# A linear-attention and gated-MLP kernel: when two weight loads, one query product and two blocks of h are issued

## The chip, the cores and the metric

The kernel runs on one core of a Trainium2 chip. The metric is device microseconds of one execution, the median of several runs. The core has a matrix engine (PE; its weight loads are listed as PEld), a vector engine (DVE), a scalar engine (ACT), GpSimd (POOL) and SyncE (SP). Each engine executes its own instructions in the order in which they were written. Here SP and ACT also issue DMAs: SP's run on queue q1, ACT's on q10, both on the core's 16 DMA engines.

## The reference

For x of 2048 x 576 (one batch), all in fp32:

```
phi(t) = where(t > 0, t + 1, exp(t)) + 1e-6
kv  = sum over s of phi(k)[s] v[s]          # 32 heads of 18
z   = sum over s of phi(k)[s]
a   = (phi(q) kv / (phi(q) z + 1e-6)) @ wo
b   = (gelu(x @ w_gate) * (x @ w_up)) @ w_down     # 576 -> 4608 -> 576
g   = sigmoid((x * gate_w).sum(-1))
out = g * a + (1 - g) * b
```

## The kernel before

**Arithmetic.** Every operand of a product is split in two parts, high and low; a product is three matmuls (high by high, high by low, low by high). The large products of the MLP follow a scheme of seven products for a 2 x 2 block product, with sums of blocks made beforehand; `f`, `e`, `u`, `p` are the buffers in which DVE combines the seven results.

**Stages.** Until about 134 us keys, values and their grams are made. Then `states` (L445 to L454) multiplies `wv` with the grams, for five slices kt; each slice needs its split of `wv`, the low part of which POOL makes (L424). `key_sums_mm` (L461 to L465) is ten matmuls with two columns each. `query(b, g)` (L427 to L437) is 14 matmuls 512 wide for block b and head group g, then two activations on ACT and one DVE operation. `wo_load` (L513) brings a slice of `wo`, splits it on ACT and POOL; `states_out` (L521) takes the states out of PSUM; the result meets `wo` at L551. Until 285 us PE does the attention: for each of 16 row tiles `mixed(b, t)` (L671) runs 30 matmuls on `p`, the split of scaled queries (`scaled`, L662 and L68/L69), for which DVE needs `rb`, the reciprocals of the denominators, stored to HBM (L646) and loaded back broadcast (L650) by SP. The result is copied by ACT to a buffer `ga` (L686) and stored on ACT's queue (L688); there are two `ga` buffers.

**Gate and up.** From 258 to 1109.5 us come 72 chains (`CHAINS`, `gu_steps`), numbered c0 to c71, gate or up, each seven products of seven matmuls (L828), 11.5 us. A chain other than the first runs its products in the order s1, s6, s7, s5, s2, s4, s3. The result of s1 is copied by ACT to `p` (L869); s2 accumulates on the same bank and so waits for that copy. s3 accumulates on s5's bank and waits for the DVE operation that reads it (L860 in a gate chain, L863 in an up chain). A gate chain writes `e` or `f`, with a GELU on ACT (L850, L880); an up chain multiplies into it (L853) and SP stores the blocks to `h_d` (L856). Gate weights are in `W[0]` (`wg`), up weights in `W[1]` (`wu`): the first ones are loaded ready-made from `wp_d` (2240 KB each), the later ones are fetched raw (`stage<-wgu`, L832), summed by POOL (L283) and split by ACT and POOL (`w_split`, L841 to L843). In chains 0 to 3, `s_make` (L1010 to L1014) splits sums of x that SP loads from `xsum_d` to `f` (L1008).

**Into the down stage.** With LAST = 71, chain LAST - 1 is the last gate chain (c70), LAST - 2 the last but one up chain (c69). Its weights for the last up chain (`last_up`, in the room of x's first blocks, printed as `xo`) are loaded on ACT's queue at c69 (L1047). The first down weights are fetched raw by `d_fetch(0)` (1728 KB, L971) and split by `d_make` (L977, L979). `h_load(j)` (L992, 768 KB) brings back a block of h from HBM on SP; `h_make(j)` (L997 ACT, L998 DVE) splits it. The tables `D_AT` and `H_AT` say behind which product (c, i) of the chain loop (L1028) these are issued; i counts from 0, so i = 1 is s6, i = 3 is s5, i = 5 is s4. From 1109.5 us the down stage (L1092) runs 84 units of 36 matmuls.

The order of instructions on each engine is the order of the program's text (a manual schedule).

## Time and profile before

| | |
|---|---|
| median of 3 runs | 1513.2 us (1511.0 to 1515.54) |
| profiled execution | 1515.58 us |
| its span in the trace | 1513.8 us |
| its mean granted PE clock | 0.996 |
| PE busy | 1500.9 us (99%) |
| DVE, POOL, ACT busy | 1003.3, 718.7, 546.2 us |
| PE's longest waits | 3.1 and 1.9 us for ACT's p, 0.8 for DVE's f |

In rows of the timeline the columns are start, duration, engine, line, operation, out<-in, shapes, and in brackets the idle time before the instruction with what ended it. A DMA's row on SPq or ACTq is its issue; in the chain of waits a DMA's row is the transfer up to its landing.

### The profile page before, as it was taken

The numbers are of one execution on the slowest core, as the hardware profiler recorded it, in microseconds if no ns is written. First come the engines' busy times: TensorE is split into PE (matmuls) and PEld (weight loads), VectorE is DVE, ScalarE is ACT, GpSimd is POOL, SyncE is SP. The second block draws the span as 40 slices with busy tenths as digits, with TensorE's granted clock in tenths as the row PEclk, the third lists the DMA queues.
The fourth block names the chain that finished last, engine by engine and source line by source line (L and its number), as shares of the span: only waits on it lengthen the run. The fifth ranks groups of instructions, "written<-read, shape, count | busy, mean of one in ns | idle before, by whom it ended". The sixth has DMA issues, their size and how long they took to land.

```text
span 1513.8 us, 21594 instructions
## 1 busy us (share of the span) xinstructions
PE 1500.9 (99%) x8354; PEld 1323.3 (87%) x8354; DVE 1003.3 (66%) x1324; ACT 546.2 (36%) x711; POOL 718.7 (47%) x516
## 2 busy tenths in 40 slices
PE   9999999999999999999999999999999999999999
PEld 8998889887888888888888888888789999999999
DVE  7886776385666556666556665556677767777775
ACT  6554545333222332222332222332244344444431
POOL 1674532156644644644644644543357354644620
PEclk9999999999999999999999999999999999999999
DMA  7563374662332223332223332223877656565564
GB/s 248 164 204 117 148 256 166 231 259 91 139 133 96 105 101 123 139 126 97 105 98 132 140 123 100 105 93 116 308 274 281 213 168 214 167 214 177 204 200 135
DMA packets 98494, 246.36 MB, mean 163 GB/s; under 512 B 9040, under 2 KB 36328, under 8 KB 95960
## 3 DMA queue, kind: packets, MB, share of 16 engines
q1 hardware_dynamic: 95368, 233.13, 44.2%
q10 hardware_dynamic: 3024, 11.86, 2.2%
q8 instruction: 65, 1.06, 0.3%
q14 instruction: 37, 0.30, 0.1%
HBM read 156.72 MB, written 88.24 MB: 162 GB/s over the span
## 4 chain that ended last, share of the span: by engine, by line
PE 91%; DVE 3%; issue 2%; ACT 2%; DMA 1%; POOL 1%; SPq 0%; ACTq 0%; POOLq 0%; DVEq 0%
PE bank L828 53%; PE bank L1092 26%; PE bank L433 3%; PE pair L681 2%; PE pair L199 2%; PE kpair L244 1%; PE pair L244 1%; PE kpair L199 1%; DMA ga_d<-ga 1%; POOL wv L424 1%; PE den L573 0%; DMA raw<-wk 0%; DVE f L853 0%; ACT p L68 0%; DVE r L662 0%
## 5 line engine op out<-in xcount | busy, mean ns | idle before, releaser
L828 PE MATMUL bank<-xo,wg 128*128 128x512 f32 x1764 | 414.3, 395 | 1.3 <-DVE f L860 0.8
L828 PE MATMUL bank<-xo,wu 128*128 128x512 f32 (+1 forms) x1715 | 403.4, 396 | 3.1 <-ACT p L869 3.1
L828 PEld LDWEIGHTS bank<-xo,wg 128*128 128x128 f32 x1764 | 332.1, 188 | 79.5 <-DVE e L860 1.4
L828 PEld LDWEIGHTS bank<-xo,wu 128*128 128x128 f32 (+1 forms) x1715 | 324.4, 189 | 79.0 <-ACT p L869 3.6
L1100 DVE SCALAR_TENSOR_TENSOR acc<-bank,gate,acc 128x288 f32<-128x288 f32 x288 | 140.5, 512 | 71.0 <-PE bank L1092 70.2
L283 POOL TENSOR_TENSOR stage<-stage 128x384 f32<-128x384 f32 x132 | 155.0, 1195 | 46.1 <-DMA stage<-wgu 43.5
L869 ACT ACTIVATE p<-bank 128x512 f32<-128x512 f32 x72 | 43.0, 597 | 333.9 <-PE bank L828 324.7
L842 POOL TENSOR_TENSOR wg<-stage,wg 128x768 fp32r<-128x768 f32 (+1 forms) x34 | 72.9, 2144 | 185.6 <-ACT wg L841 184.3
L842 POOL TENSOR_TENSOR wu<-stage,wu 128x768 fp32r<-128x768 f32 (+1 forms) x34 | 80.2, 2359 | 149.0 <-ACT wu L841 147.7
L1092 PE MATMUL bank<-wd,xo 128*128 128x288 f32 x1008 | 135.8, 294 | 0.0
L1092 PEld LDWEIGHTS bank<-wd,xo 128*128 128x128 f32 x1008 | 134.1, 188 | 0.0
L979 POOL TENSOR_TENSOR xo<-stage,xo 128x432 fp32r<-128x432 f32 x44 | 64.7, 1493 | 117.2 <-ACT xo L977 117.2
L874 DVE TENSOR_TENSOR u<-bank,p 128x512 f32<-128x512 f32 x72 | 49.5, 687 | 94.1 <-PE bank L828 88.8
L1092 PE MATMUL bank<-xo 128*128 128x288 f32 x792 | 107.1, 295 | 0.1
L1092 PEld LDWEIGHTS bank<-xo 128*128 128x128 f32 x792 | 105.7, 188 | 0.5 <-DVE u L863 0.4
L979 POOL TENSOR_TENSOR wd<-stage,wd 128x432 fp32r<-128x432 f32 x40 | 59.6, 1515 | 90.5 <-ACT wd L977 90.5
L860 DVE TENSOR_TENSOR f<-bank,u 128x512 f32<-128x512 f32 x54 | 37.3, 691 | 76.7 <-PE bank L828 76.5
L860 DVE TENSOR_TENSOR e<-bank,u 128x512 f32<-128x512 f32 x54 | 37.1, 691 | 74.1 <-PE bank L828 73.9
L850 ACT ACTIVATE f<-f 128x512 f32<-128x512 f32 x54 | 34.2, 633 | 143.8 <-DVE f L860 143.8
L984 POOL TENSOR_TENSOR stage<-stage 128x432 f32<-128x432 f32 x48 | 77.2, 1635 | 0.0
L888 DVE TENSOR_TENSOR u<-bank,u 128x512 f32<-128x512 f32 x72 | 49.8, 692 | 35.9 <-PE bank L828 33.6
L850 ACT ACTIVATE e<-e 128x512 f32<-128x512 f32 x54 | 34.1, 633 | 91.2 <-DVE e L860 90.8
(192 smaller groups left out, 2347.6 us busy)
## 6 DMA issues: line engine op xcount, KB each, us to landing
h_d<-sx SPq DMA_DIRECT2D x108, 256.0 KB
stage<-wgu SPq DMA_DIRECT2D x34, 768.0 KB
xo<-h_d SPq DMA_DIRECT2D x29, 768.0 KB
e<-h_d SPq DMA_DIRECT2D x28, 768.0 KB
hraw<-h_d SPq DMA_DIRECT2D x27, 768.0 KB
h_d<-e SPq DMA_DIRECT2D x72, 256.0 KB
h_d<-f SPq DMA_DIRECT2D x72, 256.0 KB
stage<-wdn SPq DMA_DIRECT2D x6, 1728.0 KB
```

The lines of the kernel that those rows point to most:

```text
L199: nc.tensor.matmul(out_t[:, :n], xa, kvw[i][:rows, r, lo:lo + n], start=(k == 0), stop=(k == 13))
L283: nc.gpsimd.tensor_tensor(o, a, b, OP.subtract)
L828: nc.tensor.matmul(ps, w_, x_, start=start and i == 0, stop=i == 6, skip_group_check=not start)
L842: nc.gpsimd.tensor_tensor(w[:, i, 3:5], src[:, :, 0:2], f32(w[:, i, 0:2]), OP.subtract)
L850: nc.scalar.activation(es[i], es[i], AF.Gelu_apprx_tanh)
L860: nc.vector.tensor_tensor(es[i], a, b, OP.add)
L874: nc.vector.tensor_tensor(u2, b, p1, OP.add)
L888: nc.vector.tensor_tensor(u3, c, u2, OP.add)
L979: nc.gpsimd.tensor_tensor(w[:, 1, c], src[:, c], f32(w[:, 0, c]), OP.subtract)
L984: nc.gpsimd.tensor_tensor(draw[:, o, c], draw[:, x, c], draw[:, y, c], OP.subtract)
L1092: nc.tensor.matmul(y, h[:, hl, g, t * 128:(t + 1) * 128], w[:, wl, g * 288:(g + 1) * 288], start=k in (1, 5) and n == 0, stop=n == len(ops ...
L1100: nc.vector.scalar_tensor_tensor(o, y, gate[:, 1, st:st + 1], o, op0=OP.mult, op1=OP.add)
```

## The change

There are four edits. `query(2, 3)` moves from behind the two `wo_load` calls to between `states(3)` and `states(4)`. The load of the first up weights into `W[1]` moves from ACT's queue, behind the first `mixed(1, t)`, to SP's, right behind the last load of reciprocals. In `H_AT` the splits of the first two h blocks move from behind s5 and s4 of the last gate chain to behind s6 and s5, and the load of the second h block moves four products later in c69. `d_fetch(0)` moves from the second product of c68 to the first of c67.

```
--- before.py
+++ after.py
@@ -490,8 +490,10 @@
     nc.vector.reciprocal(gate[:, 0], gate[:, 0])
     nc.vector.tensor_scalar(gate[:, 1], gate[:, 0], -1.0, 1.0, op0=OP.mult, op1=OP.add)
     query(2, 2)
-    for kt in range(2, 5):
-        states(kt)
+    states(2)
+    states(3)
+    query(2, 3)
+    states(4)
     key_sums_mm(rs)
     made.close()
     values.close()
@@ -575,7 +577,6 @@
 
     wo_load(0)
     wo_load(1)
-    query(2, 3)
     states_out()
     key_sums()
     query(2, 4)
@@ -805,6 +806,7 @@
     scaled_parts(0, 3)
     reciprocal(1, 1)
     reciprocals_load(1, 1)
+    nc.sync.dma_start(f32(W[1]), wp_d[1])
     mixed(0, 2)
 
 
@@ -928,8 +930,6 @@
     for t in range(BT):
         if t + 1 < BT:
             scaled(1, t + 1)
-        if t == 1:
-            nc.scalar.dma_start(f32(W[1]), wp_d[1])
         mixed(1, t)
     mixing.close()
     first_pairs.close()
@@ -1020,7 +1020,7 @@
     D_AT = {(LAST - 2, 0): lambda: d_make(0, 0), (LAST - 2, 4): lambda: d_sum(T1), (LAST - 1, 0): lambda: d_sum(T2),
             (LAST - 1, 2): lambda: d_make(0, 1), (LAST - 1, 4): lambda: d_make(0, 2), (LAST - 1, 6): lambda: d_sum(T3),
             (LAST, 4): lambda: d_sum(T4)}
-    H_AT = [(LAST - 1, 3), (LAST - 1, 5)]
+    H_AT = [(LAST - 1, 1), (LAST - 1, 3)]
     at = {}
     for n in range(1, NF2):
         for m in range(2):
@@ -1045,11 +1045,10 @@
                 nc.sync.dma_start(f32(W[0]), wp_d[0])
             if i == 0 and c == LAST - 2:
                 nc.scalar.dma_start(f32(last_up), wp_d[1])
-            if (c, i) == (LAST - 3, 1):
+            if (c, i) == (LAST - 4, 0):
                 d_fetch(0)
-            if (c, i) == (LAST - 2, 0):
-                h_load(0)
-                h_load(1)
+            if c == LAST - 2 and i in (0, 4):
+                h_load(i // 4)
             if (c, i) in D_AT:
                 D_AT[c, i]()
             if (c, i) in H_AT:
```

On PE, behind the fourth slice of the states (`pair<-gt,wv` and `bank<-gt,wv` are states, `bank<-xo,qw` a query, `bank<-ones,rs` the key sums), before:

```order
L454 MATMUL pair<-gt,wv 126x126
L452 MATMUL bank<-gt,wv 72x144
L454 MATMUL bank<-gt,wv 72x72
L465 MATMUL bank<-ones,rs 126x2 x8
L465 MATMUL bank<-ones,rs 72x2 x2
L433 MATMUL bank<-xo,qw_121 126x512 x7
L433 MATMUL bank<-xo,qw_122 126x512 x7
L433 MATMUL bank<-xo,qw_121 72x512 x7
L433 MATMUL bank<-xo,qw_122 72x512 x7
```

and in the change:

```order
L454 MATMUL pair<-gt,wv 126x126
L452 MATMUL bank<-gt,wv 72x144
L454 MATMUL bank<-gt,wv 72x72
L433 MATMUL bank<-xo,qw_121 126x512 x7
L433 MATMUL bank<-xo,qw_122 126x512 x7
L452 MATMUL pair<-gt,wv 126x252
```

The 14 matmuls of `query(2,3)`, the first two query rows, have moved from behind the key sums to ahead of the last slice of the states.

On SP, at the last loads of reciprocals (`rb`), before:

```order
L650 DMA rb<-rden_d_66 126x1x1280
L646 DMA rden_d_67<-rb 35x256
L650 DMA rb<-rden_d_67 126x1x1280
L1008 DMA f<-xsum_d_73 128x1024
L1008 DMA f<-xsum_d_74 128x1024
L832 DMA stage<-wgu 128x1536
L1008 DMA f<-xsum_d_75 128x1024
```

and in the change:

```order
L651 DMA rb<-rden_d_66 126x1x1280
L647 DMA rden_d_67<-rb 35x256
L651 DMA rb<-rden_d_67 126x1x1280
L809 DMA wu<-wp_d_97 128x4480
L1008 DMA f<-xsum_d_73 128x1024
L1008 DMA f<-xsum_d_74 128x1024
L834 DMA stage<-wgu 128x1536
L1008 DMA f<-xsum_d_75 128x1024
```

The load `wu<-wp_d` now stands between the reciprocals and the loads of `f`; on ACT's queue, where it stood between a split of `p` and the next `ga` copy, it is gone.

On SP, at the end of c69's predecessor and in c69 (`e_3197` is the second raw buffer of h, `sx` and `f` are stored blocks of an up chain), before:

```order
L1045 DMA wg<-wp_d_96 128x4480
L971 DMA stage<-wdn 128x3456
L856 DMA h_d_5_103<-e_3197 128x512
L856 DMA h_d_5_103<-e_2873 128x512
L856 DMA h_d_5_103<-sx 128x512 x2
L856 DMA h_d_5_103<-e_3197 128x512 x2
L856 DMA h_d_5_103<-sx 128x512
L992 DMA xo<-h_d_1_99 128x1536
L992 DMA e_3197<-h_d_1_99 128x1536
L856 DMA h_d_5_109<-f 128x512 x2
L856 DMA h_d_5_109<-sx 128x512 x2
```

and in the change:

```order
L971 DMA stage<-wdn 128x3456
L1045 DMA wg<-wp_d_96 128x4480
L858 DMA h_d_5_103<-e_3197 128x512
L858 DMA h_d_5_103<-e_2873 128x512
L858 DMA h_d_5_103<-sx 128x512 x2
L858 DMA h_d_5_103<-e_3197 128x512 x2
L858 DMA h_d_5_103<-sx 128x512
L992 DMA xo<-h_d_1_99 128x1536
L858 DMA h_d_5_109<-f 128x512 x2
L992 DMA e_3197<-h_d_1_99 128x1536
L858 DMA h_d_5_109<-sx 128x512 x2
```

`stage<-wdn`, the first down weights, has moved ahead of `wg<-wp_d`, and the two stores of `f` ahead of the second load of h.

On DVE, in the last gate chain (L874, L888 and L860 are `u`, `u` and `f` of s6, s7, s5, s2.. in turn; L998 is the split of h), before:

```order
L874 TENSOR_TENSOR u_2871<-bank,p_2870 128x512
L888 TENSOR_TENSOR u_2872<-bank,u_2871 128x512
L860 TENSOR_TENSOR f<-bank,u_2872 128x512
L998 TENSOR_TENSOR xo<-xo 128x1536
L860 TENSOR_TENSOR f<-bank,u_2872 128x512
L998 TENSOR_TENSOR xo<-e_3197,xo 128x1536
L860 TENSOR_TENSOR f<-bank,u_2871 128x512
```

and in the change, where L876, L890 and L862 are the same operations:

```order
L876 TENSOR_TENSOR u_2871<-bank,p_2870 128x512
L998 TENSOR_TENSOR xo<-xo 128x1536
L890 TENSOR_TENSOR u_2872<-bank,u_2871 128x512
L862 TENSOR_TENSOR f<-bank,u_2872 128x512
L998 TENSOR_TENSOR xo<-e_3197,xo 128x1536
L862 TENSOR_TENSOR f<-bank,u_2872 128x512
L862 TENSOR_TENSOR f<-bank,u_2871 128x512
```

The two L998 stand two products sooner each.

More of the change, by code (lines that the diff above doesn't have):

```diff
@@ L492, in tile_gated_mix @@
     query(2, 2)
-    for kt in range(2, 5):
-        states(kt)
+    states(2)
+    states(3)
+    query(2, 3)
+    states(4)
     key_sums_mm(rs)
@@ L577, in tile_gated_mix @@
     wo_load(1)
-    query(2, 3)
     states_out()
@@ L807, in tile_gated_mix @@
     reciprocals_load(1, 1)
+    nc.sync.dma_start(f32(W[1]), wp_d[1])
     mixed(0, 2)
@@ L930, in tile_gated_mix @@
             scaled(1, t + 1)
-        if t == 1:
-            nc.scalar.dma_start(f32(W[1]), wp_d[1])
         mixed(1, t)
@@ L1022, in tile_gated_mix @@
             (LAST, 4): lambda: d_sum(T4)}
-    H_AT = [(LAST - 1, 3), (LAST - 1, 5)]
+    H_AT = [(LAST - 1, 1), (LAST - 1, 3)]
     at = {}
@@ L1047, in tile_gated_mix @@
                 nc.scalar.dma_start(f32(last_up), wp_d[1])
-            if (c, i) == (LAST - 3, 1):
+            if (c, i) == (LAST - 4, 0):
                 d_fetch(0)
-            if (c, i) == (LAST - 2, 0):
-                h_load(0)
-                h_load(1)
+            if c == LAST - 2 and i in (0, 4):
+                h_load(i // 4)
             if (c, i) in D_AT:
```

## The prediction

> **What bounds the kernel now.** I read the busy shares first, then what PE waited for, then the granted clock in short windows. The page's first part has one engine that is nearly always busy:

> ```profile
> PE 1500.9 (99%) x8354; PEld 1323.3 (87%) x8354; DVE 1003.3 (66%) x1324; ACT 546.2 (36%) x711; POOL 718.7 (47%) x516
> ```

> The change takes no matmul away and adds none, so it can win only PE's idle time and time in which PE ran below its full clock. The waits of PE (us in total, times, longest) name the first:

> ```profile
> PE bank L828 <- ACT p L869: 5.0, 2, 3.1
> PE bank L828 <- DVE f L860: 0.8, 1, 0.8
> PE pair L454 <- POOL wv L424: 0.4, 1, 0.4
> ```

> The 5.0 are 3.1 near 300 us and 1.9 near 1103; the 0.8 lies at 1092, the 0.4 at 142. Each sits at a place that the diff touches. The second kind shows in windows of 3.41 us (columns: length; busy us of PE, PEld, DVE, ACT, POOL; granted clock; DMA share; GB/s):

> ```profile
> 141.01:144.42 3.41, 3.00 (x29) 2.80 (x29) 3.21 (x4) 1.29 (x3) 3.41 (x3) 1.00 0.99 366
> 144.42:147.84 3.42, 3.42 (x10) 2.63 (x10) 0.00 (x0) 0.00 (x0) 0.62 (x1) 0.50 0.84 289
> 294.60:298.01 3.41, 2.25 (x10) 1.51 (x8) 1.76 (x3) 1.58 (x2) 0.00 (x0) 1.00 0.65 222
> 298.01:301.42 3.41, 1.44 (x6) 1.22 (x7) 2.13 (x4) 2.61 (x4) 0.36 (x1) 1.00 0.92 351
> 301.42:304.84 3.42, 3.42 (x9) 2.69 (x9) 2.50 (x4) 0.94 (x1) 3.26 (x3) 0.50 0.29 120
> 1100.15:1103.56 3.41, 1.53 (x8) 0.90 (x7) 2.23 (x3) 1.11 (x2) 3.41 (x3) 1.00 0.36 86
> 1103.56:1106.98 3.42, 3.42 (x10) 2.64 (x9) 2.80 (x5) 0.00 (x0) 0.70 (x1) 0.50 0.40 165
> ```

> Three stretches of 3.41 us run at half the clock, each directly behind a window in which PE stood idle (1.97 us at 298, 1.88 at 1100) or ran short and tiny matmuls around an idle of 0.41 (at 141). 1.16 us of idle in 294.60:298.01 brought none. Half the clock for 3.41 us loses 1.71 us of work, three times 5.12. So what is to be had is 0.41 + 3.13 + 0.75 + 1.88 = 6.17 us of idle and 5.12 of clock, 11.3 in all.

> [...]

> **The query between the states (place A).** PE waits for the third split of `wv`, on POOL:

> ```profile
> 138.67 3.63 POOL L424 TENSOR_TENSOR wv<-raw,wv 128x576 fp32r<-128x576 f32 x2 [0.86 <-ACT wv L423]
> 142.35 0.33 PE L454 MATMUL pair<-gt,wv 128*126 128x126 f32 x1 [0.41 <-POOL wv L424]
> 143.31 1.14 PE L465 MATMUL bank<-ones,rs 128*126 128x2 f32 x10
> 144.31 14.78 PE L433 MATMUL bank<-xo,qw 128*126 128x512 f32 x56
> ```

> The same 14 matmuls of `query(2,3)` now stand ahead of states(4). Undisturbed, 56 of them take 14.78 − 1.71 = 13.07 us, so 14 take 3.27: states(4) moves from 141.6 to 144.8, while POOL is done at 142.3. The 0.41 is gone with 2.5 us to spare, and nothing is issued anew. Query's two activations now stand ahead of the two `wos` copies on ACT, 1.3 us of an engine that waits for them anyway; the first user of `wos` is head_out behind the query matmuls, at 158.9. The half-speed stretch: the window behind the moved states(4), 144.42:147.84, would hold the tiny key-sum matmuls and no idle. I take it as gone (−1.71); both ends stay, 0 and −1.71, since the ten 128x2 matmuls may count as idle whatever stands around them. Place A: −2.1, at least −0.4.

> **The first up weights (place B).** Here stands a chain from a store to PE; the first two rows are of the chain of waits, then ACT, then PE:

> ```profile
> 278.40 10.69 DMA ga_d<-ga
> 289.94 2.29 DMA ga_d<-ga
> 274.80 0.42 ACTq L932 DMA_DIRECT2D wu<-wp_d x1
> 289.17 0.74 ACT L686 ACTIVATE ga<-pair,gate 128x576 f32<-128x576 f32 x1 [6.83 <-DMA ga_d<-ga]
> 299.35 0.58 ACT L869 ACTIVATE p<-bank 128x512 f32<-128x512 f32 x1
> 285.39 5.01 PE L828 MATMUL bank<-xo,wg 128*128 128x512 f32 x21
> 299.98 4.29 PE L828 MATMUL bank<-xo,wu 128*128 128x512 f32 x12 [3.13 <-ACT p L869]
> ```

> The store of ga issued at 278.40 needs 10.69 us because 2.29 MB of up weights were put on the same queue at 274.80; a store alone takes 2.29. With only two ga buffers, the last ga copy waits until 289.17, ACT is in order, and `s_make(0)`, `s_make(1)`, the GELUs and the p copy that chain 1's second product needs come behind it. Once the load has left that queue, the last copy starts when PE has ended mixed(1,3), at about 285.5, which is 3.65 us sooner. From there to the p copy ACT and DVE work by turns with no other wait of length, so p is ready near 299.93 − 3.65 = 296.3; PE, done at 299.98 − 3.13 = 296.85, finds it. Margin 0.5 us. The idle falls away (−3.13), and with it the half stretch (−1.71).

> What the load does on SP's queue: it is issued right behind the last broadcast of reciprocals.

> ```profile
> 266.58 0.76 SPq L650 DMA_DIRECT2D rb<-rden_d x1
> 273.29 0.83 DVE L662 SCALAR_TENSOR_TENSOR r<-r,rb 126x640 f32<-126x640 f32 x1 [0.49 <-DMA rb<-rden_d]
> 288.97 4.05 POOL L283 TENSOR_TENSOR stage<-stage 128x384 f32<-128x384 f32 x4 [27.51 <-DMA stage<-wgu]
> 329.65 2.39 POOL L1014 TENSOR_TENSOR xo<-f,xo 32x1024 fp32r<-32x1024 f32 x1 [1.11 <-ACT xo L1013]
> ```

> The broadcast lands at 273.2, 6.6 us after its issue. If one queue serves in order, the weights behind it cost it nothing; that is the value I take. At 366 GB/s (the row of 141.01) they need 6.3 us and are in by some 280, where PE wants them at 290.2; the two loads of `f` behind them come by 282, wanted at 288.7. If the weights' packets instead share the engines with the broadcast, it lands up to 6.3 us later. That is the upper bound, and it goes to a rival. POOL's sums of the next weights (288.97) come sooner, not later.

> Some is given back, since chain 2 moves 4.84 us forward and what ACT and POOL prepare for it moves only 3.65: its weight splits end 1.2 us later against PE, and the small part of POOL's L1014 (ending at 332.04, needed by chain 4 about 332.4) is as tight. Bounds 0 and 1.2 + 0.8; I take 0.5, nearer to nothing, as splits feed later products of a chain too. Place B: −4.84 + 0.5 = −4.3.

> **The last gate chain (place C).** On SP, DVE, ACT and PE, in this order:

> ```profile
> 1083.91 0.32 SPq L992 DMA_DIRECT2D e<-h_d x1
> 1084.32 0.86 SPq L856 DMA_DIRECT2D h_d<-f x2
> 1087.88 0.69 DVE L888 TENSOR_TENSOR u<-bank,u 128x512 f32<-128x512 f32 x1
> 1091.90 0.69 DVE L860 TENSOR_TENSOR f<-bank,u 128x512 f32<-128x512 f32 x1 [3.33 <-PE bank L828]
> 1093.16 1.47 ACT L997 ACTIVATE xo<-xo 128x1536 fp32r<-128x1536 f32 x1
> 1094.67 1.76 DVE L998 TENSOR_TENSOR xo<-xo 128x1536 fp32r<-128x1536 f32 x1 [2.08 <-ACT xo L997]
> 1092.65 1.89 PE L828 MATMUL bank<-xo,wg 128*128 128x512 f32 x7 [0.75 <-DVE f L860]
> 1102.98 6.72 PE L828 MATMUL bank<-xo,xo 128*128 128x512 f32 x21 [1.88 <-ACT p L869]
> ```

> The 3.33 us ahead of L860 is put down to PE, but its product (s5, the fourth of a chain begun at 1081.9, 7 × 0.23 = 1.62 us each) was there by 1088.4, and DVE was free at 1088.6. What came last is the store of `f` that must leave before L860 writes it again: issued at 1084.32 behind the load of the second h block, which itself waited on SP until 1083.91. In the change the `f` stores stand ahead of that load, so L860 no longer waits for it. The h splits (L997 1.47, L998 1.76 to 2.08) come two products sooner: the first between the L874 and the L888 of this chain, the second behind the first L860.

> New is a wait of ACT and DVE for the first h block. If it lands at t, DVE reaches s5's L860 at t + 1.47 + 2.08 + 0.69, ends it 0.69 later: t + 4.9. PE needs that at 1092.65 − 0.75 = 1091.9 less some 0.1 of signalling. **Turning point: t = 1086.9.** Why I expect less, from SP, ACT and the DMA queues in 1074:1080:

> ```profile
> 1059.86 0.37 SPq L971 DMA_DIRECT2D stage<-wdn x1
> 1073.64 0.93 ACT L977 ACTIVATE xo<-stage 128x864 fp32r<-128x864 f32 x1 [0.79 <-DMA stage<-wdn]
> 1074.97 0.59 SPq L992 DMA_DIRECT2D xo<-h_d x1
> q10 hardware_dynamic: 106, 1.90, 86.5%
> q1 hardware_dynamic: 114, 0.22, 9.5%
> ```

> The block is issued at 1074.97, while the last up weights (2.29 MB, q10, from 1072.26) take nearly all; they are through by about 1081. Then 0.79 MB and the remaining 0.2 MB of stores take 2.8 us at 353 GB/s: t is near 1084.5. With the down weights fetched a chain sooner (1.77 MB from about 1047.3, while the queues stand empty), the load of `wg` at 1059 and all that follows it on SP has less ahead. The second h block, issued behind two stores, is in by 1089 to 1090; its split ends near 1095, and p of the last chain is ready near 1097.5, where PE asks at 1102.98 − 1.88 = 1101.1. So −0.75 − 1.88 and −1.71 for the clock: −4.3. Lower end: nothing more; upper end −1.5, if t comes 3 us late.

> [...]

> **Sum.** −2.1 − 4.3 − 4.3 = −10.7, against the profiled execution's 1515.58: 1504.9. That execution lay 2.4 above the median of 1513.2, which may itself have held a half stretch fewer, so I say **1504.6**; alone this case spans 1501.5 to 1508.

> **Rivals.**
> - *The halved clock stays.* The drops come at those places whatever PE's idle, and only 6.2 us less 0.5 go: 1509.9. Against it: the rows show each drop right behind idle. 0.08. [...]
> - *Place B gives back what it gets.* The weights' packets hold up the broadcast: DVE's L662 of 273.29 comes up to 6.3 later, and mixed(1,2) waits 3 to 4.8 us and draws a half stretch, or the chains 2 to 4 wait for splits. B comes to nothing: 1509.2. For it: a margin of 1.2 us only at mixed(1,2), the load wholly ahead of the `f` loads. Against: one queue, in order. 0.15.
> - *Slower.* The first h block stays at the share that q1 had above: 0.22 MB in 6 us is 37 GB/s, so 0.79 MB need 21 us and land at 1096.3, 9.4 after the turning point. With a half stretch that is 11.1 of new loss at C against its 4.3 before: 1515.58 − 6.4 + 6.8 = 1516.0. Each further us of delay costs one; from t = 1098 on it is slower than the median by over 0.3%. Against it: the stretch at 9.5% ends with the 2.29 MB. 0.06.
> - *The change doesn't do what it says*: ga's copy still waits, as the stores share 16 engines with the same bytes later; B's idle shrinks to some 1.5 us and the drop stays: 1508. 0.06.

> **How the numbers follow.** The forecast has 0.65, the rivals 0.08, 0.15, 0.06 and 0.06. Within 0.3% (4.5 us, about what a measurement here can tell) of 1513.2 means 1508.7 to 1517.7. Faster: the forecast, the last rival and a part of B's, 0.76; within: 0.19; slower: 0.05. The range of 1500.5 to 1511 takes in the first two rivals, and below it more gain than the sum, if the run has yet other drops.

> **What would show it.** Right: no wait of PE for ACT's p, no `DMA ga_d<-ga` ahead of L686, clock 1.00 in every window from 135 on, L860 of the last gate chain within 1 us of its product. Wrong: a wait of PE at mixed(1,2) for p, of chain 2 for POOL's splits, or of chain 70 for L860 behind L998; a 0.50 window that follows no idle.

## The result and the profile after

The changed kernel takes 1505.59 us (median of 6 runs, 1504.8 to 1508.17), the kernel before 1513.36 in the same comparison (1509.97 to 1515.54). The ratio is 0.9955 (95% interval 0.9941 to 0.9969): by that ratio it is 6.8 us faster, between 4.7 and 8.9, and the two medians lie 7.8 apart. The profiled execution took 1506.67, with a span of 1504.9 against 1513.8. Line numbers shift by a few from kernel to kernel: the product at L828 of before is L830 here.

PE's busy time, and its longest waits behind the first ten microseconds:

```profile
PE 1496.2 (99%) x8354; PEld 1320.3 (88%) x8354; DVE 1010.0 (67%) x1324; ACT 545.9 (36%) x711; POOL 718.7 (48%) x516
```

```profile
PE bank L830 <- DVE e L862: 1.3, 2, 0.8
...
PE pair L682 <- ACT p L68: 1.1, 1, 1.1
```

The three rows of waits that the prediction showed have gone, the one for ACT's p with 5.0 us among them. Two waits are new: one of 0.8 for DVE's e near 311 (the other 0.5 of that row stood before as well, near 362) and one of 1.1 for a split p. The granted clock is 1.00 in every window up to the last matmul (it falls at 1503.83, behind it); the three places, in windows of 4 us:

```profile
142.00:146.00 4.00, 4.00 (x26) 3.40 (x24) 1.33 (x4) 0.88 (x2) 0.28 (x1) 1.00 0.92 353
299.00:303.00 4.00, 4.00 (x19) 3.28 (x18) 3.93 (x4) 0.60 (x1) 3.84 (x3) 1.00 0.53 184
1098.00:1102.00 4.00, 4.00 (x24) 3.54 (x23) 3.19 (x5) 0.40 (x1) 0.00 (x0) 1.00 0.35 131
```

PE at the stations that were compared (start, duration):

```profile
156.59 0.96 PE L553 MATMUL pair<-wos,kvt 126*126 126x288 f32 x6
268.01 16.58 PE L682 MATMUL pair<-kw,p 126*128 126x288 f32 x120 [1.05 <-ACT p L68]
289.28 11.46 PE L830 MATMUL bank<-xo,wu 128*128 128x512 f32 x49
300.57 10.26 PE L830 MATMUL bank<-xo,wg 128*128 128x512 f32 x42
311.63 1.89 PE L830 MATMUL bank<-xo,wg 128*128 128x512 f32 x7 [0.80 <-DVE e L862]
313.36 11.46 PE L830 MATMUL bank<-xo,wu 128*128 128x512 f32 x49
1077.19 11.64 PE L830 MATMUL bank<-xo,wg 128*128 128x512 f32 x49
1100.15 10.12 PE L1091 MATMUL bank<-xo 128*128 128x288 f32 x72
```

Against the same stations of before (158.93, 269.10, 290.24, 306.50, chain 3 at 318.08, 1081.89, 1109.54) PE is ahead by 2.34, 1.09, 0.96, 5.93, 4.72, 4.70 and 9.39 us, and by 8.9 at the end. The differences of neighbours are what each stretch brought:

| stretch | predicted | profile after against before |
|---|---|---|
| place A, the query between the states | -2.1 | -2.34 |
| up to mixed(1,0) and chain 1 | 0 | +1.38 |
| place B, up to the start of chain 2 | -4.84 | -4.97 |
| chain 2 | +0.5 | +1.21 |
| place C | -4.3 | -4.69 |
| down stage | 0 | +0.5 |
| sum | -10.7 | -8.9 |

Place B on ACT:

```profile
280.96 0.74 ACT L687 ACTIVATE ga<-pair,gate 128x576 f32<-128x576 f32 x1 [2.50 <-DMA ga_d<-ga]
284.63 0.74 ACT L687 ACTIVATE ga<-pair,gate 128x576 f32<-128x576 f32 x1 [2.92 <-PE pair L682]
294.60 0.58 ACT L871 ACTIVATE p<-bank 128x512 f32<-128x512 f32 x1
```

The last ga copy now waits for PE, no longer for a store. The copy before it does wait 2.50 for one: the store issued at 273.38, beside the weights on the other queue (issued at 267.45), lands some 7.5 us later (a store alone took 2.29 in the profile of before), while the DMA engines are busy all the time (share 1.02 from 274 to 278). So the weights still hold up the stores, only earlier, where ACT has time. Place C, on ACT and DVE:

```profile
1080.37 1.49 ACT L997 ACTIVATE xo<-xo 128x1536 fp32r<-128x1536 f32 x1 [0.74 <-DMA xo<-h_d]
```

```profile
1081.89 1.76 DVE L998 TENSOR_TENSOR xo<-xo 128x1536 fp32r<-128x1536 f32 x1
1083.57 0.68 DVE L890 TENSOR_TENSOR u<-bank,u 128x512 f32<-128x512 f32 x1
1084.34 0.69 DVE L862 TENSOR_TENSOR f<-bank,u 128x512 f32<-128x512 f32 x1
```

The first h block lands at 1080.3; with PE's advance of 4.7 us that is 1085.0 on the old scale (1084.5 expected, turning point 1086.9). L862 runs within 1 us of its product (1077.19 + 4 × 1.62 = 1083.7).

### The profile page after: what moved, and what is told of

Its sections match the earlier page's. It is cut to its first block, busy times and chain, and to the rows that moved or that the text cites. A ratio compares the mean times of both kernels' runs of the same rounds, so it can differ in the third digit from the quotient of the medians.

```text
span 1504.9 us, 21594 instructions
## 1 busy us (share of the span) xinstructions
PE 1496.2 (99%) x8354; PEld 1320.3 (88%) x8354; DVE 1010.0 (67%) x1324; ACT 545.9 (36%) x711; POOL 718.7 (48%) x516
## 4 chain that ended last, share of the span: by engine, by line
PE 90%; DVE 3%; DMA 2%; issue 2%; ACT 2%; POOL 1%; SPq 0%; ACTq 0%; DVEq 0%; POOLq 0%
PE bank L830 52%; PE bank L1091 24%; PE bank L433 4%; PE pair L244 2%; PE pair L682 2%; PE kpair L244 2%; PE pair L199 2%; PE kpair L199 2%; DMA stage<-wdn 1%; DMA rb<-rden_d 1%; DMA xo<-h_d 0%; DVE r L663 0%; POOL wd L979 0%; ACT p L68 0%; DMA raw<-wk 0%
## 5 line engine op out<-in xcount | busy, mean ns | idle before, releaser
L830 PE MATMUL bank<-xo,wg 128*128 128x512 f32 x1764 | 414.4, 395 | 1.5 <-DVE e L862 1.3
L830 PEld LDWEIGHTS bank<-xo,wg 128*128 128x128 f32 x1764 | 332.0, 188 | 79.8 <-DVE e L862 2.2
L830 PE MATMUL bank<-xo,wu 128*128 128x512 f32 (+1 forms) x1715 | 401.5, 394 | 0.0
L830 PEld LDWEIGHTS bank<-xo,wu 128*128 128x128 f32 (+1 forms) x1715 | 323.3, 189 | 75.1
L283 POOL TENSOR_TENSOR stage<-stage 128x384 f32<-128x384 f32 x132 | 156.2, 1204 | 45.6 <-DMA stage<-wgu 43.0
L844 POOL TENSOR_TENSOR wg<-stage,wg 128x768 fp32r<-128x768 f32 (+1 forms) x34 | 72.9, 2145 | 182.0 <-ACT wg L843 180.7
L844 POOL TENSOR_TENSOR wu<-stage,wu 128x768 fp32r<-128x768 f32 (+1 forms) x34 | 79.9, 2349 | 149.1 <-ACT wu L843 147.9
L876 DVE TENSOR_TENSOR u<-bank,p 128x512 f32<-128x512 f32 x72 | 49.5, 687 | 93.5 <-PE bank L830 92.3
L979 POOL TENSOR_TENSOR wd<-stage,wd 128x432 fp32r<-128x432 f32 x40 | 59.4, 1510 | 91.5 <-ACT wd L977 91.5
L862 DVE TENSOR_TENSOR f<-bank,u 128x512 f32<-128x512 f32 x54 | 37.2, 691 | 73.4 <-PE bank L830 73.1
L862 DVE TENSOR_TENSOR e<-bank,u 128x512 f32<-128x512 f32 x54 | 37.1, 691 | 72.5 <-PE bank L830 72.2
L890 DVE TENSOR_TENSOR u<-bank,u 128x512 f32<-128x512 f32 x72 | 49.8, 692 | 36.5 <-PE bank L830 34.2
L682 PEld LDWEIGHTS pair<-kw,p 126*128 126x128 f32 (+1 forms) x480 | 65.1, 188 | 3.4 <-ACT p L68 1.7
```

The source lines that it names most:

```text
L283: nc.gpsimd.tensor_tensor(o, a, b, OP.subtract)
L682: nc.tensor.matmul(y[:, i, :288], p[:R, a, g], KW[g][:R, wl, i * 288:(i + 1) * 288], start=(n == 0), stop=(n == 14))
L830: nc.tensor.matmul(ps, w_, x_, start=start and i == 0, stop=i == 6, skip_group_check=not start)
L844: nc.gpsimd.tensor_tensor(w[:, i, 3:5], src[:, :, 0:2], f32(w[:, i, 0:2]), OP.subtract)
L862: nc.vector.tensor_tensor(es[i], a, b, OP.add)
L979: nc.gpsimd.tensor_tensor(w[:, 1, c], src[:, c], f32(w[:, 0, c]), OP.subtract)
```

## The experiments

Ratios are to the kernel before, timed beside each run on the same chip; its medians there were 1512.4 to 1512.9. A time in us behind a ratio is that ratio's distance from 1 times 1513.

**Each place alone.** The query only:

```
-    for kt in range(2, 5):
-        states(kt)
+    states(2)
+    states(3)
+    query(2, 3)
+    states(4)
...
-    query(2, 3)
     states_out()
```

> The kernel before with query(2,3) between the states, nothing else. Theory (idle and half-speed stretches are what is won, and part is handed back by the reciprocals of block 1): PE reaches head_out (L551) 2.1 to 2.4 us sooner than before's 158.93, no window of 0.50 clock near 145, but a new PE wait of about 1.0 us for the split p of mixed(1,0) near 268, so that chain 0 and all behind it come only 1.0 to 1.3 us sooner: about 1512.2. Rival 1 (nothing is handed back): 1511.1 and no wait at mixed(1,0). Rival 2 (the half-speed stretch does not hang on the 0.41 us of idle): only 0.4 us, 1512.9, with a 0.50 window near 145.

Measured: 1511.86, ratio 0.9994 (0.9984 to 1.0003), 0.9 us faster, with zero inside the interval. The expected wait at mixed(1,0) did not come, so that the query hands something back there falls as a theory.

The first up weights only, on SP's queue:

```
     reciprocals_load(1, 1)
+    nc.sync.dma_start(f32(W[1]), wp_d[1])
...
-        if t == 1:
-            nc.scalar.dma_start(f32(W[1]), wp_d[1])
```

> The kernel before with the first up weights on SP's queue, nothing else. Theory: the wait of 3.13 us for ACT's p near 300 and the half-speed stretch behind it go (-4.8), a wait of 0.5 to 0.8 us for DVE's e in chain 2 is added, nothing waits at mixed(1,0): about 1509.3. Rival (the weights' packets hold up the reciprocals' broadcast on the same queue): the broadcast rb lands later than 273.3, mixed(1,2) waits, and the time stays within 1 us of before, 1512.5 to 1514. Rival (clock does not follow the gap): 1510.5 with a 0.50 window near 302.

Measured: 1511.18, ratio 0.9986 (0.9977 to 0.9994), 2.1 us faster. The wait for p near 300 is gone and chain 2 waits 0.50 and 0.82 instead, but about half of what was expected arrives.

The third and fourth edit only (`H_AT`, `h_load`, `d_fetch` as in the diff):

> The kernel before with the third and fourth edit only (h splits two products sooner, second h load behind the f stores, first down weights a chain ahead). Theory: both PE waits near 1092 and 1103 and the half-speed stretch go, -4.3 to -4.7 up to the start of the down stage, about 0.5 lost again behind it: about 1509.2; the waits at 142 and 300 stay. Rival (the clock does not follow the gap): 1510.7 with a 0.50 window near 1104. Rival (the first h block lands late): a wait of PE for L860 in the last gate chain, 1510 to 1513.

Measured: 1509.95, ratio 0.9977 (0.9968 to 0.9987), 3.5 us faster. Both waits at place C are gone. But its profile holds two surprises: no half-speed stretch follows the wait of 3.10 us for p near 300, and chain 2, in which nothing was changed, waits as in the changed kernel (PE):

```profile
299.72 5.17 PE L828 MATMUL bank<-xo,wu 128*128 128x512 f32 x21 [3.10 <-ACT p L869]
308.38 6.95 PE L828 MATMUL bank<-xo,wg 96*128 96x512 f32 x29 [0.44 <-POOL wg L843]
316.14 1.91 PE L828 MATMUL bank<-xo,wg 128*128 128x512 f32 x7 [0.81 <-DVE e L860]
```

**When a gap halves the clock.** Windows set on the edges of the half stretches, first of the run with the query alone, then of the run with the weights alone:

```profile
293.67:297.08 3.41, 1.00 (x4) 0.86 (x5) 2.12 (x4) 2.17 (x4) 0.00 (x0) 1.00 0.89 341
297.08:300.50 3.42, 3.42 (x9) 2.67 (x8) 2.94 (x4) 1.37 (x2) 3.19 (x2) 0.50 0.45 182
1095.80:1099.22 3.42, 2.30 (x10) 1.54 (x10) 2.03 (x5) 1.11 (x2) 3.11 (x3) 1.00 0.68 212
```

```profile
140.62:144.03 3.41, 3.03 (x28) 2.78 (x28) 2.99 (x4) 1.10 (x2) 3.41 (x3) 1.00 1.01 357
144.03:147.44 3.41, 3.41 (x10) 2.65 (x9) 0.00 (x0) 0.00 (x0) 0.40 (x1) 0.50 0.93 319
1096.35:1099.76 3.41, 1.52 (x7) 0.93 (x6) 2.12 (x4) 1.12 (x2) 3.41 (x3) 1.00 0.50 132
1099.76:1103.18 3.42, 3.42 (x10) 2.64 (x9) 2.53 (x4) 0.00 (x0) 0.36 (x1) 0.50 0.40 157
```

The two stretches of the second run begin 955.73 us apart, which is 280.0 times 3.413, the length of a half stretch in the trace's clock records. The three of the kernel before (at 144.42, 301.43 and 1103.56) lie 46.0 and 235.0 times that apart, and the fall behind the last matmul there, at 1513.16, lies 120.0 times that behind the third. So in each of these two profiles the falls lie on one grid of 3.413 us, and its offset differs from execution to execution (a line lies at 297.08 in the run with the query, at 298.01 in the kernel before). In these profiles a grid window of 128x512 matmuls with 1.53 us of busy PE or less was followed by half the clock (1.00 and 1.52 here, 1.45 and 1.53 in the kernel before); one with 2.25 or 2.30 was not.

The run of place C alone has a gap of 3.10 us. Its clock next falls at 1509.64, behind the last matmul. With 3.4133 us a window (955.73 / 280) the grid line 355 windows before that lies at 297.91 and cuts the gap in two:

```profile
294.50:297.91 3.41, 2.12 (x10) 1.40 (x8) 1.76 (x3) 1.58 (x2) 0.00 (x0) 1.00 0.71 222
297.91:301.32 3.41, 1.60 (x7) 1.34 (x8) 2.02 (x5) 2.77 (x4) 0.52 (x1) 1.00 0.94 347
```

With 2.12 and 1.60 us of busy PE both windows hold more than the 1.53 above, and no half stretch follows (the clock is 1.00 in 302:306 too). So a gap of 3.13 us was followed by half the clock in one profile, the kernel before, and one of 3.10 in this one was not. For the 1.9 us at place C the runs have no such pair: it halved the clock in both profiles that show it, and the window with 2.30 belongs to a shorter gap there, 1.12 us. Of the three half stretches that I counted, the profiled execution had all. Of the two places that each run had left unchanged, the run with the query had one, that with the weights both, and that of place C none.

**The changed kernel without the query:**

```
     states(2)
     states(3)
-    query(2, 3)
     states(4)
...
     wo_load(1)
+    query(2, 3)
     states_out()
```

> The changed kernel with query(2,3) put back behind the loads of wo. Theory: the 0.41 us wait for POOL and the half-speed stretch at 145 are back (+2.1 to +2.4), but the 1.05 us wait at mixed(1,0) is gone, so it is only 1.0 to 1.3 slower than the change: about 1506.8. Rival (the wait at mixed(1,0) comes from the weights on SP's queue, not from PE coming sooner): the wait stays near 1 us and the time is about 1507.9.

Measured: 1507.37, ratio 0.9961 (0.9949 to 0.9972). That is 0.3 us from the changed kernel's 0.9959 of the next run and 0.9 from the 0.9955 of the first comparison, within the intervals. In its profile place A's wait is back (0.40) without a half stretch, and there is no wait at mixed(1,0); the next run shows that the latter says little.

**The changed kernel once more:**

> The changed kernel once more, beside the other kernels of this group. Theory now (from the runs so far: a gap halves the clock only when it fills enough of one window of a free-running 3.41 us grid, so the kernel before pays between none and three half stretches): 1505 to 1506.5, its runs closer together than those of before, since no gap over 1.1 us is left. If the changed kernel had half stretches by chance too, its runs would spread as far as before's (some 7 us).

Measured: 1506.86 (1506.13 to 1507.71), ratio 0.9959 (0.9946 to 0.9971). The five runs lie within 1.6 us, the six of the first comparison within 3.4, and the 23 runs of before beside these five within 6.5 (1509.53 to 1516.06). Its profile has chain 2's waits again (0.52 and 0.81), no half stretch, no wait at mixed(1,0), and one of 0.27 at mixed(1,2): the 1.05 us belong to one execution, not to the change.

**The first split earlier:**

```
-                w_split(m)
+                w_split(m, (1,) if c == 1 else (0, 1))
...
                 s_load(k + 2)
+                if k == 1:
+                    w_split(0, (0,))
```

(`w_split` takes the halves to be split as a second argument here.)

> The changed kernel, and the first half of the first weight split (ACT L843, POOL L844) moved from behind the p copy of chain 1 to behind the second s_make. Theory: chain 2's wait for POOL's split goes, and POOL's half split no longer lies beside DVE's work of chain 1, so chain 2's wait for DVE's e near 311 shrinks from 0.8 to under 0.4: 0.4 to 1.2 faster than the change, about 1505.0. Rival (the 0.8 us come from DVE being full with its own operations, whatever POOL does): the wait for e stays at 0.7 or more, or grows as PE reaches it sooner, and the time is that of the change.

In this kernel the split stands ahead of chain 0's last product, which then reads the new weights: that part of the computation is changed. Measured: 1513.58, ratio 1.0003 (0.9994 to 1.0012): PE waited 6.1 us for the split (PE's waits), and two half stretches came with it, from 291.8 to 298.6.

```profile
PE bank L830 <- ACT wg L843: 6.1, 1, 6.1
```

The edit answers nothing on the time, but its DVE rows do on the cause. The same operation of chain 1 stands first in this run, where POOL is idle beside it, then in the run of place C alone:

```profile
308.65 0.69 DVE L855 TENSOR_TENSOR e<-u,e 128x512 f32<-128x512 f32 x1
```

```profile
303.15 0.68 DVE L853 TENSOR_TENSOR e<-bank,e 128x512 f32<-128x512 f32 x1
304.46 2.71 DVE L853 TENSOR_TENSOR e<-u,e 128x512 f32<-128x512 f32 x1
```

The 2.71 lies beside POOL's L842 (304.19 to 306.63). Five operations of chain 1 (L853, L902, L914) take 1.21 to 2.71 there, 5 us more than at 0.69 each, and so DVE comes late to chain 2. The 0.68 lies beside POOL too (L843, 302.75 to 304.11), but that operation reads a `bank`, a tile in PSUM. All of the changed kernel's trace agrees (DVE's TENSOR_TENSOR on 128x512, 280 to 1110 us): with a `bank` among the inputs they take 0.67 to 0.69 whether POOL's TENSOR_TENSOR runs beside them or not; without one, 0.68 to 0.69 alone and 0.68 to 2.70 beside POOL, half of them about 1.4 or more.

**Place C without the earlier down weights** (`H_AT` and `h_load` alone):

> The kernel before with the third edit only: h splits sooner, second h load behind the f stores; the first down weights stay where they were. If the f stores ahead of the h load are what frees L860 (my reading), both PE waits of 0.75 and 1.88 us are gone here as in the run with both edits, about 1510. If the first h block needs the earlier down weights to land in time, PE waits for L860 in the last gate chain behind L998 by 1 us or more.

Measured: 1509.92, ratio 0.9980 (0.9970 to 0.9990), as with both edits. The fourth edit has no effect on the time that these runs can tell. What it does stands in the profile: without it ACT waits for the first h block.

```profile
1086.02 1.49 ACT L997 ACTIVATE xo<-xo 128x1536 fp32r<-128x1536 f32 x1 [2.87 <-DMA xo<-h_d]
```

Chain 70 begins at 1080.71 here, 1.18 ahead of before, so the block lands at 1087.2 on the old scale, 2.2 us later than in the changed kernel and at the turning point. Chain 70 takes 11.77 us instead of 11.48. Near 300 this profile has the wait of 2.86 with a half stretch, and no wait in chain 2: the slow stretch covers it.

**Many tiny matmuls:**

```
     key_sums_mm(rs)
+    for at in range(420, 500, 20):
+        key_sums_mm(rs, at)
```

(`at` is the column of the bank to which the sums go.)

> The changed kernel with the ten 128x2 matmuls of the key sums repeated four times more into unused columns of the same bank (some 4.0 us of PE, without idle between). If only idle PE halves the clock: no 0.50 window near 146 to 155 and +4.0 us. If such small matmuls count as idle: a window of 3.41 us at 0.50 right behind them, +5.7 us.

Measured in a single execution: 1515.38, with a span of 1513.5, 8.4 us over the 1505.1 of the changed kernel timed beside it. PE is never idle here:

```profile
146.00:149.80 3.80, 3.80 (x40) 3.80 (x39) 0.69 (x1) 1.14 (x2) 2.77 (x2) 1.00 0.56 197
149.80:153.21 3.41, 3.41 (x14) 2.60 (x15) 1.25 (x6) 0.71 (x2) 0.00 (x0) 0.51 0.00 0
153.21:156.63 3.42, 3.42 (x9) 1.90 (x8) 2.77 (x13) 0.78 (x2) 0.00 (x0) 0.50 0.00 0
```

The fifty 128x2 matmuls take 5.80 us from 145.50 on. The first half stretch begins while they still run, at 149.9, behind a grid window filled with them, and a second follows at once: a window filled with 128x2 matmuls was followed by half the clock, though PE is listed as busy throughout (3.80 of 3.80 us up to 149.80). The 40 added ones (4.7 us) and twice 1.71 make 8.1 of the 8.4; one half stretch was expected. So at place A the ten of them (1.14 us) may have counted beside the 0.41 us of idle. What decides there is not shown: in the run of place C the wait of 0.40 and all ten lie in one grid window (140.90 to 144.31), and no half follows.

**The changed kernel without the weights' move:**

```
     reciprocals_load(1, 1)
-    nc.sync.dma_start(f32(W[1]), wp_d[1])
...
+        if t == 1:
+            nc.scalar.dma_start(f32(W[1]), wp_d[1])
```

> The changed kernel with the first up weights back on ACT's queue. Theory now (the half stretch at 302 of the profile before covered chain 2's waits for POOL's split and DVE's e, 1.2 to 1.3 us together; what the weights' move wins is the 3.1 us of idle and, by chance, a half stretch, less that): 1.8 to 3.0 slower than the change, 1508.0 to 1509.5, with the wait of about 3 us for p near 297 and no wait over 0.6 in chain 2 if a half stretch follows, 1.2 us of them if not. Rival (the weights' move is worth the 4.3 us of the prediction): 1510 to 1511.

Measured: 1509.08 (1505.8 to 1510.44), ratio 0.9978 (0.9969 to 0.9987): the weights' move is worth about 0.9978 − 0.9959 = 0.0019, 2.9 us, or 3.5 against the 0.9955 of the first comparison (each ratio is known to some 0.001). The profiled execution happened to be the fastest, 1505.8, and in it the wait for p is absent though the weights are on ACT's queue (its chain of waits):

```profile
276.24 7.14 DMA ga_d<-ga
...
284.51 2.08 DMA ga_d<-ga
```

The store took 7.14 us instead of 10.69, and the last ga copy was on time. So the 3.1 us, too, are not in every execution.

**One low part on POOL:**

```
         nc.scalar.activation(X[1][:, S2:S1 + 1, kt, c], raw, AF.Copy)
+        if k == 1:
+            eng = nc.gpsimd
         eng.tensor_tensor(X[1][rows, S2:S1 + 1, lo, c], raw[rows], f32(X[1][rows, S2:S1 + 1, kt, c]), OP.subtract)
```

> The changed kernel with the low part of the second s_make (1.23 us on DVE, near 292) made on POOL, which stands idle from 290.8 to 296.3. If chain 2's two waits come from DVE's and ACT's chain of chain 0 and 1 (DVE full, the split behind the p copy), p and the split come 1.0 to 1.2 sooner: POOL's wait of 0.5 goes, the wait for e falls from 0.8 to 0.3 or less, 1.0 to 1.3 faster than the change: about 1505.2. Rival (DVE's operations are stretched by POOL's work beside them, not by their number): the wait for e stays at 0.6 or more.

Measured: 1504.57 (1503.91 to 1505.08), ratio 0.9950 (0.9938 to 0.9963). Its interval overlaps that of the change. POOL's wait in chain 2 is gone, that for e is 0.27:

```profile
309.85 1.89 PE L830 MATMUL bank<-xo,wg 128*128 128x512 f32 x7 [0.27 <-DVE e L862]
```

The rival, that the stretching alone keeps this wait at 0.6 or more, did not come. The same five operations of chain 1 still take 1.08 to 1.81 here, 4 us more than at 0.69 each, but DVE starts on chain 1 1.3 us sooner against PE. So the wait had both causes: POOL's work beside DVE, and DVE's own work ahead of it.

**Reciprocals and gate weights earlier.** On top of that:

```
-    nc.scalar.dma_start(f32(W[0]), wp_d[0])
+    nc.sync.dma_start(f32(W[0]), wp_d[0])
...
     scaled(0, 2)
+    reciprocal(1, 0)
+    reciprocals_load(1, 0)
...
     scale(0, 3)
-    reciprocal(1, 0)
-    reciprocals_load(1, 0)
```

> The kernel before this one and two edits more: the first gate weights on SP's queue instead of ACT's, and the reciprocals of block 1, half 0, ahead of a 1.9 us copy on ACT. If the waits of 0.3 to 1.1 us at mixed(1,0) seen in some profiles come from reciprocals that land late (8.2 us for the load, ga stores behind the gate weights), they go: 0.3 to 0.8 faster than the run before, about 1504.7. Rival: the second broadcast, behind mixed(1,1), is what is late then, and nothing more is won.

Measured: 1506.64, ratio 0.9963 (0.9951 to 0.9976). On SP the load is issued at 236.59, ahead of three ga stores. The store issued at 240.00 takes 12.56 us though the weights are on the other queue; ACT waits for it, and PE for ACT:

```profile
252.64 0.74 ACT L687 ACTIVATE ga<-pair,gate 128x576 f32<-128x576 f32 x1 [5.92 <-DMA ga_d<-ga]
```

```profile
254.57 6.10 PE L682 MATMUL pair<-kw,p 126*128 126x288 f32 x30 [1.66 <-ACT p L68]
```

PE runs at half the clock from 255.47 to 258.88 here, behind a grid window with 1.68 us of busy PE, in matmuls 288 wide.

Without the gate weights' move, the reciprocals alone:

> The run with the low part on POOL, and of the two further edits only one: the reciprocals of block 1, half 0, ahead of the 1.9 us copy on ACT; the first gate weights stay on ACT's queue. If those weights on SP's queue, issued at 236.6 instead of 242.8, were what made the run with all three slower, it is back at 1504.0 to 1504.8, with no wait at 254. If the reciprocal's new place was, it stays near 1506.5.

Measured: 1504.14 (1503.13 to 1505.33), ratio 0.9947 (0.9934 to 0.9961), the fastest kernel of the study by its median; its interval overlaps that of the change. It has no wait at 254 and none for a split p. So by the profiles the gate weights' place was at fault; the intervals of the two runs overlap.

## Why the prediction was right, and where its sizes were off

The mechanisms were right: at all three places the wait named went, by the step named, and the time of 1505.59 lies 1.0 from the forecast. Profile against profile the sum gave 1504.9 and 1506.67 came, 1.8 more; that the median lies closer is in part luck. Point by point:

- **Place A** was sized as 0.41 of idle and a half stretch of 1.71. In the profiles this is right (2.34). Over many executions it is worth less: 0.9 us alone, 0.3 to 0.9 as the difference of the changed kernel with and without it, none of these clear of zero. Of the profiles with the query in its old place, two have the half stretch there (before, and the weights alone) and three have not.
- **Place B**'s step to the p copy at 296.3 was right (ready at 295.18 with PE 0.96 ahead, which is 296.14). Mis-sized is what is given back: 0.5 was taken, 1.21 measured, and the bound of 1.2 + 0.8 held it. The half stretch of before had covered these waits, as the run of place C alone shows, which has the gap but no half stretch, and waits 0.44 and 0.81 in chain 2. That DVE's operations took up to 2.71 us beside POOL's splits instead of 0.69 was not in the sum at all. Over executions B is worth 2.1 us alone and 2.9 to 3.5 as a difference, not 4.3.
- **Place C** came as forecast, 4.69 in the profile. For the wait of 0.75 the `f` store was the cause: in the profile of before the store issued at 1084.32 lands at 1091.8, behind the second h block (1091.1), and L860 begins at 1091.90. The stores' new order and the earlier splits are one edit, and no run has one without the other. The sentence on the down weights ("has less ahead") held: without that edit the first h block landed at the turning point instead of 1.9 ahead of it. That was worth 0.3 us of PE in one profile, too little for the medians to tell.
- **The clock** is the step of the sum that was off in kind: three half stretches, 5.12 us, were counted as part of the kernel, with a doubt of one for the median. At places A and B the half stretch came in some profiles and not in others; at place C it came in both profiles that have the gap of 1.9 us. The sum against the profiled execution, −10.7, was therefore larger than what the comparison found, 6.8 by the ratio and 7.8 between the medians. The number forecast stayed close because neither profile of the changed kernel has a half stretch. The edits alone add up to this: 0.9 + 2.1 + 3.5 = 6.5.
- **Rivals.** That the half stretch stays did not happen. The slower case did not: the first h block landed 1.9 before its turning point. The last one was right in part: a ga copy still waits 2.50, but not the last. The broadcast behind which the weights stand does land later, 266.60 to 274.37 (DVE's L663) against 266.58 to 273.29; that one queue serves in order, so that the weights cost the broadcast nothing, was an assumption, and by these two landings they may have cost it up to 1.1 us. But mixed(1,2) waited only 0.27 to 0.72 in the profiles where it waited at all. Two signs that were named for being wrong did come, both small: in the second profile of the change mixed(1,2) waits 0.27, and chain 2 waits 0.52 for POOL's split, which is part of what place B gave back.

Two losses stay open. The wait of 1.05 at mixed(1,0) stands in one of two profiles of the changed kernel. DVE waits there for the reciprocals' load, which took 8.23 us from 258.10; why it was slow is not shown. The last two runs issue these reciprocals earlier and do not have the wait, but other runs without that edit do not have it either. Of the 0.5 lost in the down stage 0.2 is a wait for DVE's acc; the rest no view shows.

## What to carry to other kernels

Before counting a half-speed stretch as time to be won, place the gap on the grid of 3.413 us on which the falls lay: a gap of 3.1 us cost 1.7 us on top of itself in some executions here and nothing in another, so one profile overstates or hides it. Ask of every slow stretch what it covers: work on other engines that catches up during it becomes the next wait when it is gone (0.44 and 0.81 us in chain 2 here). A large load on the queue of small stores is best issued where the stores' consumer has slack; changing the queue alone was not enough here: beside the load on the other queue a store still took some 7.5 us in the changed kernel and 12.56 in another run, against 2.29 alone.
